# Sigmoid attention and a GELU feed-forward on one core: half of each k load issued on GpSimd's queue instead of SyncE's

## The chip, the core and the metric

The kernel runs on one core of a Trainium2 chip. The metric is device time in microseconds (us) for one execution, and lower is better. A core has TensorE (PE in the profile; its weight loads are a row of their own, PEld), VectorE (DVE), ScalarE (ACT), GpSimd (POOL) and SyncE (SP). Each runs its own instructions in order and waits for the others by semaphores. DMAs are issued on the queue of SP, ACT or POOL, and the transfers of all three are carried by the same 16 DMA engines. In the profile SP's transfers are queue q1, ACT's q10 and POOL's q0.

## The reference

```python
def _attn_ref(q, k, v):                      # each (8, 12, 448, 64), float32
    S = q.shape[2]
    scale = 1.0 / np.sqrt(q.shape[-1])
    scores = scale * np.matmul(q, k.transpose(0, 1, 3, 2)) - np.log(S)
    attn = 1.0 / (1.0 + np.exp(-scores))     # a sigmoid, no softmax
    return np.matmul(attn, v)

x = attn_out.transpose(0, 2, 1, 3).reshape(8 * 448, 768)
h = x @ w_in                                 # (768, 2048)
g = 0.5 * h * (1.0 + erf(h / sqrt(2)))       # exact GELU
out = g @ w_out                              # (2048, 768)
```

## The kernel before, in words

**Two stages.** The attention stage (`attention`) fills the first 240 us or so, and the feed-forward (`feed_forward`), which is the rest, reads attention's result back from a scratch tensor in DRAM, `scr_x`. While attention runs, a `Decoder` unpacks the weights (stored as 64-bit words) a step at a time with VectorE and ScalarE, and writes them to scratch tensors (`scr_f`, later `scr_out`).

**Units.** Attention's work is cut into 24 units, B x NU = 8 batches x 3, each with two pairs of heads. A head pair lies in the 128 partitions: head j = 0 in partitions 0 to 63, head j = 1 in 64 to 127. One tile `qk` holds a unit's q and k (`raw[:, pp, 0]` is q and `raw[:, pp, 1]` is k), and there are three such buffers. So the load of unit u + 3 can start only when unit u's buffer has been read for the last time.

**One unit on the engines.** `scores` multiplies k by q on TensorE into PSUM (line 380; from unit 1 on as three products of high and low parts), and `sigmoid` turns each of six chunks into a tile `a` on ScalarE (line 358). `values` multiplies `a` by v (line 413), computes the last 64 keys of the *next* unit on the way (`scores_tail`, line 397, which reads `qk` as loaded), and goes on with the values. `park` copies the result to a tile `x` on VectorE (line 452) and stores it to `scr_x` on POOL (line 455). The high and low parts are made from `qk` as it was loaded: the high part by `high_qk` on ScalarE up to unit 17 for the first head pair, otherwise on VectorE (line 341), the low part on VectorE (line 350).

**What sets the order.** The scheduling is by hand: each engine runs its instructions in the order in which the program issues them. Before the loop come `load(0)`, `load_v(0)`, `load(1)`, `load_v(1)`, `load(2)`. Then each round of the loop over u issues, in this order: the scores of unit u, `load(u + 3)`, the splits of unit u + 1 (`split_qk`), a few decoder steps, the values of unit u with the tail scores of unit u + 1 and ScalarE's split of unit u + 2 (`idle`), more decoder steps inside it, `park`, and `load_v(u + 2)`.

**The queues around the change.** `load(u)` (lines 320 and 324) issues q in one DMA of 448 KB for both pairs, and k in two of 224 KB, one for each half of the partitions (j = 0 and j = 1). All three go on SP, but for unit 0, whose loads are cut by pair and whose j = 0 half of k goes on ACT. On SP they stand in order with v's loads (line 333) and the decoder's loads of raw weights (line 114); late in attention also with loads of the decoded weights (line 243). POOL issues the decoder's stores (`scr_f`, line 156), the stores of `x` (line 455) and, once, after unit 16, four loads that bring the first part of `scr_x` back for the feed-forward (`load_x`, tile `xl`, line 286). POOL computes nothing in attention.

Of the kernel before, what the change touches and what calls it, by code (L numbers as in the profile page):

```python
# [21 lines left out]
def tile_sigmoid_attention_gelu_ffn(  # L22
# [10 lines left out]
    nc = tc.nc  # L33
# [240 lines left out]
    def rows(j):  # L274
        return slice(j * D, j * D + D)
# [31 lines left out]
    def attention(at, ps):  # L307
# [3 lines left out]
        def load(u):  # L311
            if u >= total:
                return
            b, n = divmod(u, NU)
            raw = at.tile([P, 2, 2, S], F32, tag="qk", name=f"qk{u}", bufs=3)
            for pp in (slice(0, 1), slice(1, 2)) if u == 0 else (slice(0, 2),):
                if u == 0 and pp.start == 1:
                    nc.scalar.activation(one, one, AF.Sigmoid)
                hps = slice(2 * n + pp.start, 2 * n + pp.stop)
                nc.sync.dma_start(raw[:, pp, 0], q[b, hps].rearrange("p r s -> r p s"))  # L320
                for j in range(2):
                    src = k[b, hps, rows(j), j].rearrange("p r s -> r p s")
                    queue = nc.scalar if j == 0 and u == 0 else nc.sync
                    queue.dma_start(raw[rows(j), pp, 1], src)
            raws[u] = raw

# [139 lines left out]
        for i in range(10):  # L466
            nc.tensor.matmul(warm[:, 0], ready[:, :P], ready, start=True, stop=True)  # L467
        load(0)
        load_v(0)
        load(1)  # L470
        load_v(1)
        load(2)
        for u in range(total):
            for p in range(2):
# [415 lines left out]
```

## Time and profile before

| what | value |
|---|---|
| time, median of 3 runs | 1024.78 us (1024.43 to 1025.58) |
| the profiled execution | 1025.23 us |
| its span, first to last instruction | 1023.5 us |
| mean granted TensorE clock | 1.000 |
| PE busy | 1019.0 us (100%) |
| PEld busy | 922.4 us (90%) |
| DVE busy | 785.7 us (77%) |
| ACT busy | 605.0 us (59%) |
| POOL busy | 116.7 us (11%) |
| SP's queue (q1) | 153.82 MB, 49.9% of 16 DMA engines' span |
| POOL's queue (q0) | 55.26 MB, 15.0% |
| ACT's queue (q10) | 1.72 MB, 0.5% |

How to read it: the span is the part of the execution from the first to the last instruction. The ends of matmuls are modelled, so PE's busy time says that TensorE always had work in hand and not that it ran at its peak; where it waited is seen better in PEld's rows. In the lists of waits, a row gives who waited, for whom, the total time, how often, and the longest. In the timeline, a row gives start and duration, the engine, the line and the operation, `out<-in`, and in brackets the idle time before it and what ended that. A name with q at its end, as SPq, is the engine's queue, that is, its sequencer issuing a DMA: the duration is that of the issue, not of the transfer. "To landing" is from the issue to the last byte.

### The profile page before, as it was taken

What the parts mean: (1) busy time and instruction counts of PE and PEld (TensorE: products, weight loads), DVE (VectorE), ACT (ScalarE), POOL (GpSimd) and SP (SyncE); (2) the same over time, 40 slices, a digit from 0 to 9 for tenths busy, and PEclk for the clock granted to TensorE, in tenths of its full rate; (3) what the DMA queues carried; (4) which work ended last, traced back from release to release, by engine and by line L of the source; (5) the groups of instructions that cost most, each with busy time, mean ns of one, the idle gap of its engine ahead of it and who ended that gap; (6) DMA issues with size and microseconds to landing.
All of it is one profiled execution on the core that took longest, in us unless ns stands there. A gap on an engine that the chain in (4) does not pass through costs nothing.

```text
span 1023.5 us, 16634 instructions
## 1 busy us (share of the span) xinstructions
PE 1019.0 (100%) x6478; PEld 922.4 (90%) x6478; DVE 785.7 (77%) x1011; ACT 605.0 (59%) x804; POOL 116.7 (11%) x186
## 2 busy tenths in 40 slices
PE   9999999999999999999999999999999999999998
PEld 5656666567999999999999999999999999999998
DVE  3678777885799698996688888566888875678875
ACT  5888887784445465555366645635655455466552
POOL 0111102101323362224000000100000000000000
PEclk9999999999999999999999999999999999999999
DMA  9999999996788797688444445634444553334441
GB/s 259 290 326 319 310 326 301 349 284 228 236 259 272 265 340 261 215 282 322 158 143 126 147 123 161 220 107 140 131 114 133 163 166 100 117 115 133 139 138 64
DMA packets 85935, 211.87 MB, mean 207 GB/s; under 512 B 9376, under 2 KB 35872, under 8 KB 85856
## 3 DMA queue, kind: packets, MB, share of 16 engines
q1 hardware_dynamic: 69072, 153.82, 49.9%
q0 software_dynamic: 14880, 55.26, 15.0%
q10 hardware_dynamic: 1904, 1.72, 0.5%
q8 instruction: 51, 0.84, 0.3%
q14 instruction: 28, 0.23, 0.1%
HBM read 163.38 MB, written 50.33 MB: 209 GB/s over the span
## 4 chain that ended last, share of the span: by engine, by line
PE 100%; DVE 0%; DVEq 0%; issue 0%
PE pf L525 76%; PE pav L413 12%; PE sc L380 9%; PE sc_t L397 2%; PE pav L428 0%; PE warm L467 0%; DVE tmp L562 0%; DVEq L886 0%
## 5 line engine op out<-in xcount | busy, mean ns | idle before, releaser
L525 PE MATMUL pf<-op,whl 128*128 128x448 f32 x2016 | 382.8, 353 | 0.0
L525 PEld LDWEIGHTS pf<-op,whl 128*128 128x128 f32 x2016 | 380.3, 189 | 1.8 <-DVE op L562 0.8
L254 ACT CAST whl<-wst 128x768 fp32r<-128x768 f32 x212 | 176.4, 833 | 241.8 <-PE pf L525 210.4
L525 PE MATMUL pf<-xh_p,whl 128*128 128x448 f32 x1008 | 273.4, 352 | 0.0
L261 DVE TENSOR_TENSOR whl<-wst,whl 128x768 fp32r<-128x768 f32 x212 | 201.8, 953 | 47.1 <-ACT whl L254 46.9
L525 PEld LDWEIGHTS pf<-xh_p,whl 128*128 128x128 f32 x1008 | 190.5, 189 | 0.2
L525 PE MATMUL pf<-xl_p,whl 128*128 128x448 f32 x504 | 177.6, 352 | 0.0
L358 ACT ACTIVATE a<-sc 128x896 f32<-128x896 f32 x144 | 119.3, 934 | 33.4 <-PE sc L380 33.4
L413 PE MATMUL pav<-a,v 64*64 64x448 f32 x1296 | 132.8, 541 | 0.0
L562 DVE TENSOR_TENSOR op<-g,op 128x896 fp32r<-128x896 f32 x112 | 121.4, 1085 | 5.8 <-ACT op L572 5.7
L413 PEld LDWEIGHTS pav<-a,v 64*64 64x64 f32 x1296 | 55.2, 132 | 61.2 <-issue 34.5
L572 ACT CAST op<-g 128x896 fp32r<-128x896 f32 x112 | 104.6, 935 | 2.6 <-PE pf L525 2.6
L525 PE MATMUL pf<-xh,whl 128*128 128x448 f32 x384 | 104.2, 353 | 0.0
L525 PEld LDWEIGHTS pf<-xl_p,whl 128*128 128x128 f32 x504 | 95.3, 189 | 0.0
L525 PEld LDWEIGHTS pf<-xh,whl 128*128 128x128 f32 x384 | 72.6, 189 | 0.8 <-issue 0.7
L562 DVE TENSOR_TENSOR g<-g,g 128x896 f32<-128x896 f32 x64 | 69.4, 1084 | 0.0
L525 PE MATMUL pf<-xl,whl 128*128 128x448 f32 x192 | 67.7, 352 | 0.0
L559 ACT ACTIVATE g<-tmp 128x448 f32<-128x448 f32 x72 | 45.2, 628 | 35.8 <-DVE tmp L562 35.8
L562 DVE TENSOR_TENSOR tmp<-pf,g 128x448 f32<-128x448 f32 x72 | 44.9, 624 | 27.2 <-PE pf L525 26.4
L562 DVE TENSOR_TENSOR g<-pf,g 128x448 f32<-128x448 f32 x48 | 29.9, 624 | 34.6 <-PE pf L525 34.5
L380 PE MATMUL sc<-lo,hi 64*128 64x448 f32 x276 | 51.2, 367 | 0.0
L133 ACT ACTIVATE me<-me 128x512 f32<-128x512 int32 (+1 forms) x40 | 29.5, 738 | 36.6 <-DVE me L122 36.6
(78 smaller groups left out, 910.0 us busy)
## 6 DMA issues: line engine op xcount, KB each, us to landing
wst<-scr_out SPq DMA_DIRECT2D x112, 384.0 KB, 3.2
wst<-scr_in SPq DMA_DIRECT2D x84, 384.0 KB, 3.1
v<-v_dram SPq DMA_DIRECT2D x24, 512.0 KB, 6.9
raw<-w_in_dram SPq DMA_DIRECT2D x16, 768.0 KB, 5.0
raw<-w_out_dram SPq DMA_DIRECT2D x24, 512.0 KB, 5.5
scr_x<-x POOLq DMA_DIRECT2D x24, 448.0 KB, 7.6
out_dram<-tmp SPq DMA_DIRECT2D x47, 224.0 KB, 2.3
qk<-q_dram SPq DMA_DIRECT2D x23, 448.0 KB, 9.7
```

The costliest lines, as they stand in the source:

```text
L133: nc.scalar.activation(e.bitcast(F32), e.bitcast(I32), AF.Relu, bias=1151.0 * 2**23, scale=-8.0)
L254: nc.scalar.copy(hl[:, 0], t)
L261: nc.vector.tensor_tensor(hl[:, 1], t, hl[:, 0], op=ALU.subtract)
L358: nc.scalar.activation(to, sc, AF.Sigmoid, bias=NEG_LOG_S, scale=SCALE)
L380: nc.tensor.matmul(sc[:, j], ks[rows(j), 1, keys], braid(qs[rows(j), 0]) if braided else qs[rows(j), 0], start=n == 0, stop=n == last,)
L397: nc.tensor.matmul(sc[rows(p), j], raw[rows(j), p, 1, FULL * P :], raw[rows(j), p, 0], start=True, stop=True,)
L413: nc.tensor.matmul(pav[rows(j), p], vals[u][half, p, j, c], a[p][half, j], start=not swap and c == order[0], stop=c == (order[-1], FULL - ...
L525: nc.tensor.matmul(bank, a, braid(m), **flags)
L559: nc.scalar.activation(straight(dst), unbraid(src), AF.Gelu)
L562: nc.vector.tensor_tensor(out, a, b, op=op)
L572: nc.scalar.copy(op[:, 0], src)
```

## The change

From unit 1 on, the j = 1 half of k (partitions 64 to 127, both head pairs, 224 KB) is issued on POOL's queue and not on SP's. Its place in the program, its bytes, its source and its destination are the same. Unit 0 keeps its queues: j = 0 on ACT and j = 1 on SP. q, the j = 0 half of k, and v stay on SP.

```diff
                 nc.sync.dma_start(raw[:, pp, 0], q[b, hps].rearrange("p r s -> r p s"))
                 for j in range(2):
                     src = k[b, hps, rows(j), j].rearrange("p r s -> r p s")
-                    queue = nc.scalar if j == 0 and u == 0 else nc.sync
+                    queue = (nc.scalar, nc.sync) if u == 0 else (nc.sync, nc.gpsimd)
+                    queue = queue[j]
                     queue.dma_start(raw[rows(j), pp, 1], src)
             raws[u] = raw
```

## The prediction

> **What bounds the kernel now.** I read the busy totals and the chain first, then the waits of the attention stage, then one middle unit, and last the start, where the queues fill.
>
> ```profile
> PE 1019.0 (100%) x6478; PEld 922.4 (90%) x6478; DVE 785.7 (77%) x1011; ACT 605.0 (59%) x804; POOL 116.7 (11%) x186
> PE 100%; DVE 0%; DVEq 0%; issue 0%
> PE pf L525 76%; PE pav L413 12%; PE sc L380 9%; PE sc_t L397 2%; PE pav L428 0%; PE warm L467 0%; DVE tmp L562 0%; DVEq L886 0%
> ```
>
> The chain that ended last is TensorE from end to end. A changed DMA moves the time only if it makes TensorE wait, or ends a wait that TensorE has. The moved loads end with attention, so the rows that count are the waits of the first 240 us:
>
> ```profile
> ACT a L358 <- PE sc L380: 33.4, 24, 3.9
> DVE x L452 <- PE pav L413: 23.5, 19, 2.9
> PEld pav L413 <- ACT a L358: 14.5, 64, 0.3
> DVE hi L341 <- DMA qk<-k_dram: 1.0, 1, 1.0
> PEld sc L380 <- DMA qk<-k_dram: 0.7, 1, 0.7
> ACT hi L341 <- DMA qk<-k_dram: 0.7, 1, 0.7
> ```
>
> Columns: who, whom, total us, times, longest. TensorE waited for q or k once, 0.7 us, and that was unit 0 (its row is below), whose loads the change leaves alone. The other two waits are of VectorE and ScalarE, which themselves idle 23.5 and 33.4 us for TensorE. So k's lateness costs nothing now, and the gain to be had from it is about nothing.
>
> One middle unit, whose scores begin at 86.17:
>
> ```profile
> 86.17 3.60 PE sc L380 x36
> 95.98 3.60 PE sc L380 x36
> 84.79 0.93 ACT L341 CAST hi<-qk 128x896 fp32r<-128x896 f32 x1
> 86.98 4.97 ACT L358 ACTIVATE a<-sc 128x896 f32<-128x896 f32 x6 [1.26 <-PE sc L380]
> 85.66 1.44 SPq L324 DMA_DIRECT2D qk<-k_dram  x2
> 85.54 0.56 POOL L156 DMA_DIRECT2D scr_f<-wd  x1 [6.92 <-DVE wd L147]
> 87.71 0.71 POOL L455 DMA_DIRECT2D scr_x<-x  x1 [1.61 <-DVE x L452]
> 86.26 1.16 DVE L452 COPY x<-pav 128x448 f32<-128x448 f32 x2 [1.02 <-PE pav L413]
> 88.33 0.62 DVE L341 CAST hi<-qk 128x896 fp32r<-128x896 f32 x1
> ```
>
> The period is 95.98 - 86.17 = 9.81 us, set by the scores, sigmoid, values circle; SP and POOL only have to be in time.
>
> **The change part by part.** It adds and removes no bytes. 23 of the 46 k loads of 224 KB go from SP's queue to POOL's, each past SP's v, raw and q issues, and behind POOL's `scr_f`, `scr_x` and, once, x0's loads.
>
> *SP, per unit.* One issue of about 0.72 us (1.44 for two) less. SP is not on the chain: 0.
>
> *POOL, per unit.* In program order the moved load stands behind the store of the unit before, so it is issued at 87.71 + 0.71 = 88.4 and not at about 86.4, 2 us later. Its own wait, for the third-last `qk` buffer, ends earlier: that buffer's last readers are the tail scores and splits before 86.17. So nothing is held up behind it: the next POOL item, `scr_f`, comes 9.81 us after 85.54, and POOL's 6.92 us idle ahead of that takes an issue of 0.57 to 0.71 us.
>
> *When k lands.*
>
> ```profile
> scr_x<-x POOLq DMA_DIRECT2D x24, 448.0 KB, 7.6
> qk<-k_dram SPq DMA_DIRECT2D x46, 224.0 KB, 10.5
> DMA to landing us min/median/max: 3.0/7.5/11.8
> q1 hardware_dynamic: 82, 0.45, 54.2%
> q0 software_dynamic: 77, 0.41, 49.3%
> q1 hardware_dynamic: 265, 0.43, 107.0%
> ```
>
> The third row is of all transfers of `scr_x`. The fourth and fifth are the queues in 24 to 26 us (packets, MB, share of the engines), SP's q1 beside POOL's q0; the last is q1 alone in 9 to 11 us. The store ahead lands 7.6 us after 87.71, at 95.3; 224 KB more at POOL's 0.41 MB in 2 us take 1.1 us: 96.4. SP's second half now lands at about 86.4 + 10.5 = 96.9. The first use is ScalarE's split of that unit, two periods after 84.79: 104.4. Slack 8 us; by the longest landing (88.4 + 11.8 + 1.1 = 101.3) still 3. Cost 0.
>
> *The worst unit.* x0's loads go out on POOL ahead of unit 20's k:
>
> ```profile
> 176.72 3.05 POOL L286 DMA_DIRECT2D xl<-scr_x  x4
> 177.29 0.63 DVE L341 CAST hi<-qk 128x896 fp32r<-128x896 f32 x1
> 178.97 0.55 DVE L122 TENSOR_SCALAR me<-raw 128x768 uint32<-128x768 uint32 x1
> 195.26 0.62 DVE L341 CAST hi<-qk 128x896 fp32r<-128x896 f32 x1
> 195.91 1.09 DVE L350 TENSOR_TENSOR lo<-qk,hi 128x896 fp32r<-128x896 f32 x1
> 203.84 0.19 PEld L380 LDWEIGHTS sc<-lo,hi 64*128 64x128 f32 x2 [0.70 <-issue]
> ```
>
> It is issued at 179.8 and by that longest landing is there at 192.7; VectorE splits it at 195.26, and its scores begin at 203.84. Slack 2.6 us to the split, and then 8.6 less 3.4 for the two splits (0.62 and 1.09 twice) to TensorE. Cost 0.
>
> *VectorE beside POOL's issues.* Four issues in 3.05 us ran beside a cast of 0.63 us, where the undisturbed one at 195.26 took 0.62, and were not slowed either: 0.76 each, against 0.71 for `scr_x`. The moved issue falls beside the cast at 88.33. Cost 0; the cover is the 1.02 us that VectorE idles before its next copy, and without it the issue's 0.71 us in 21 units would be 15 us.
>
> [...]
>
> *The start.* POOL has nothing to wait for there, so the second halves of units 1 and 2 (2 x 224 KB) go out at once, beside unit 0's loads, where SP sends them after unit 0.
>
> ```profile
> 0.74 0.40 SPq L320 DMA_DIRECT2D qk<-q_dram  x1
> 0.74 0.56 ACTq L324 DMA_DIRECT2D qk<-k_dram  x1
> 7.66 1.40 SPq L324 DMA_DIRECT2D qk<-k_dram  x2
> 4.59 1.25 PEld L380 LDWEIGHTS sc<-qk 64*128 64x128 f32 x5 [0.73 <-DMA qk<-k_dram]
> 10.37 0.21 PEld L397 LDWEIGHTS sc_t<-qk 64*64 64x64 f32 x8 [0.65 <-ACT a L358]
> 2.94 0.59 SPq L333 DMA_DIRECT2D v<-v_dram  x1
> v<-v_dram SPq DMA_DIRECT2D x1, 512.0 KB, 7.0
> 11.17 3.19 PE L413 MATMUL pav<-a,v 64*64 64x448 f32 x32
> 17.37 3.77 PE sc L380 x36
> ```
>
> TensorE already waits here, 0.73 us, for unit 0's k; what delays that load delays all. The engines can't be late by more than POOL's packets occupy them: 0.41 MB took 49.3% of 2 us, 0.99 us, so 448 KB (0.459 MB) take 1.10 us; if POOL's k goes in the small packets of SP's loads, by the 107% of 2 us for 0.43 MB, 2.3 us. Lower end 0: POOL's data may come after unit 0's first pair. Not below: all that is moved was queued behind that pair. Later waits of unit 0 add nothing: v lands at 9.9, 1.2 us ahead of its use at 11.17, and the second pair is covered by ScalarE, for which TensorE waits 0.65 us at 10.37. What SP loses (224 KB ahead of unit 1, at 0.43 MB in 2 us 1.07 us) pays back POOL's time by unit 1, but TensorE's shift stays. Between 0 and 2.3 I take 0.6, half the 1.10: the large packets are what POOL's row shows, and with both queues starting at once about half of them should fall ahead of the first pair.
>
> **Sum.** +0.6 us at the start, 0 elsewhere. The profiled execution took 1025.23 (span 1023.5 and 1.7 around it) and would take 1025.8; the median of the three runs, 1024.78, is 0.45 lower, so 1025.4.
>
> **The rivals.**
> Hidden altogether: POOL's first data come after unit 0's. For it: a store issued on POOL beside a full SP queue takes 7.6 us. Time 1024.8, on the same side of what a measurement can tell (0.2%, 2.05 us).
>
> Slower by the start: POOL's k goes in small packets, all ahead of the first pair. It decides above 2.05 us, so only at its end of 2.3: 1027.1. Against it: POOL's 77 packets carried 0.41 MB, 5.3 KB each, while q1's 265 carried 1.6 KB.
>
> Slower by late k: beyond its slack k makes ScalarE's split late, which pushes the sigmoids. Each us beyond the 8 of slack and the 1.26 that ScalarE idles costs 21 us over 21 units, 1046. It needs landings of 17 us; the longest on POOL was 11.8.
>
> Faster: with less queued on SP, the early loads land sooner. The 1.0 and 0.7 us waits on k go, but neither engine is on the chain; TensorE's own 0.7 us is unit 0's. At most 1024.1. Over 0.2% would need 2.05 us of TensorE waiting for loads, and the list has 0.7. Against: the 14.5 us that it waits for ScalarE, if those hang on loads by a path I don't see; a seventh of it gone gives 1022.7.
>
> [...]
>
> **How the numbers follow.** Forecast, a start cost of 0.1 to 2.05 us: 0.50. Hidden: 0.37. Slower by the start beyond 2.05: 0.07. Late k: 0.03. Faster: 0.03. Faster, same, slower: 0.03, 0.87, 0.10. The range runs from 1024.0, the lowest run 1024.43 less about its spread, to the start's upper end, 1027.1.
>
> **What would show it.** SP's k groups of one load instead of two; POOL issuing two k loads before 3 us; unit 1's scores later than 17.37 by up to 1 us; the period still 9.81; the splits' waits on k gone; the feed-forward unchanged. It is wrong if the period moves, if ScalarE's or VectorE's waits for k grow past a few us, or if TensorE gets a row of waits for `qk` after unit 0.

## The result, and the profile after

The change makes the kernel slower. The median of six runs went from 1025.13 to 1031.01 us (1029.47 to 1033.82), a ratio of 1.0059 with a 95% interval of 1.0049 to 1.0069. One of the six runs before took 5377.27 us; the ratio leaves it out, and the other five have a median of 1024.79. The profiled execution of the changed kernel took 1030.97 us with a span of 1029.2, against 1025.23 and 1023.5. Line numbers behind the edit are one higher than in the kernel before.

The page of the changed kernel gives the busy totals, and the chain that ended last by engine and line:

```profile
PE 1021.3 (99%) x6478; PEld 922.1 (90%) x6478; DVE 786.6 (76%) x1011; ACT 605.1 (59%) x804; POOL 131.6 (13%) x209
PE pf L526 73%; PE pav L414 12%; PE sc L381 8%; PE sc_t L398 2%; DMA xl<-scr_x 1%; DMA qk<-q_dram 1%; DMA scr_out<-s 1%; PE pav L429 0%; DVE xl L290 0%; ACTq L286 0%; DVE s L96 0%; ACT xh L289 0%; DVE s L95 0%; DVE s L98 0%; DVE whl L261 0%
```

POOL has its 23 further DMAs (209 instructions, not 186). The chain is no longer TensorE alone. It leaves TensorE twice: once for a load of q, and once through `xl<-scr_x`, the sums `s`, a store `scr_out<-s` and `whl`. Here is the chain in order of time, some rows of many (start, duration, what):

```profile
1.82 6.90 DMA qk<-q_dram
...
18.60 3.77 PE sc L381 x36
...
87.42 3.60 PE sc L381 x36
...
97.23 3.60 PE sc L381 x36
...
263.18 0.63 POOL scr_out L170
263.81 5.66 DMA scr_out<-s
...
269.55 0.70 DVE s L95
...
272.17 0.88 DVE whl L261
273.10 11.98 PE pf L526 x53
```

Unit 1's scores start at 18.60, where they stood at 17.37: 1.23 us later. The middle unit starts at 87.42 (86.17 before), and its period is 97.23 - 87.42 = 9.81, as before. So one part of the loss is made at the start and is carried along unchanged. Setting the starts of TensorE's instructions of both traces side by side, the shift is +1.24 us from unit 1 to the end of attention and on into the feed-forward. At one place, 269.61 us in the trace of before and 273.10 here, it jumps to +3.49, and by 274 us of before it has grown to +5.09, where it stays. What comes after TensorE's last work adds some 0.6, which makes the 5.7 of the two spans. That part differs between executions anyway (run k below, whose TensorE has no shift, has 0.48 more there than the kernel before), so it isn't put down to the change.

**What happens at 273.** The feed-forward's weights need a last step on VectorE (line 261 makes `whl`), and that stands behind VectorE's sums for the decoder's second half (`mix`, lines 95 to 98, into the one buffer `s`). Four POOL stores read `s`, and the next group's first sum must wait until the last of them has landed. These are the lists of waits from 236 to 280 us, a row of before and then the same of after:

```profile
DVE s L95 <- DMA scr_out<-s: 2.0, 1, 2.0
```

```profile
DVE s L95 <- DMA scr_out<-s: 4.6, 1, 4.6
```

In the kernel before, VectorE had `whl` ready shortly ahead of its use, as its rows show:

```profile
265.67 0.69 DVE L95 TENSOR_TENSOR s<-wd 128x512 f32<-128x512 f32 x1 [1.98 <-DMA scr_out<-s]
268.20 0.95 DVE L261 TENSOR_TENSOR whl<-wst,whl 128x768 fp32r<-128x768 f32 x1
269.61 0.19 PEld L525 LDWEIGHTS pf<-xh,whl 128*128 128x128 f32 x1
```

268.20 + 0.95 is 269.15, and the first load of these weights is at 269.61. The slack was 0.46 us. A TensorE that never waits gives no sign of it. In the changed kernel the same two instructions of VectorE, and TensorE's wait:

```profile
269.55 0.69 DVE L95 TENSOR_TENSOR s<-wd 128x512 f32<-128x512 f32 x1 [4.62 <-DMA scr_out<-s]
272.09 0.95 DVE L261 TENSOR_TENSOR whl<-wst,whl 128x768 fp32r<-128x768 f32 x1
273.10 0.19 PEld L526 LDWEIGHTS pf<-xh,whl 128*128 128x128 f32 x1 [2.24 <-DVE whl L261]
```

`whl` is 3.89 us later, 1.24 of which is the start's shift that TensorE shares; the other 2.65 less the 0.46 of slack leave 2.19 us of waiting, and the row has 2.24. Then TensorE's clock fell. This is the table by windows, whose columns are window, length, busy time and count of PE, PEld, DVE, ACT and POOL, granted clock, DMA share and GB/s:

```profile
271.00:273.00 2.00, 0.20 (x2) 0.00 (x0) 2.00 (x4) 0.00 (x0) 1.50 (x3) 1.00 0.51 145
273.00:275.00 2.00, 1.90 (x6) 1.77 (x7) 1.97 (x5) 1.51 (x3) 1.65 (x3) 0.66 0.89 243
275.00:277.00 2.00, 2.00 (x7) 1.77 (x6) 1.93 (x4) 1.19 (x3) 0.49 (x1) 0.50 1.00 371
```

Granted 0.66 and 0.50 in two windows of 2 us, TensorE lost about 2 x (0.34 + 0.50) = 1.7 us more. By the starts, 3.49 - 1.24 = 2.25 us of waiting and 5.09 - 3.49 = 1.60 of clock make the jump of 3.85.

**Why the store was late.** Here are POOL's issues around the first group of sums, in the kernel before and in the changed one. The stores are counted from the first that reads `s`; two of the group, from `wd`, go ahead of it, and the fifth is from `wd` again:

```profile
258.99 1.45 POOL L170 DMA_DIRECT2D scr_out<-s  x2 [10.65 <-issue]
260.61 1.45 POOL L170 DMA_DIRECT2D scr_out<-s  x2 [0.16 <-issue]
269.81 1.46 POOL L170 DMA_DIRECT2D scr_out<-s  x2 [1.71 <-DVE me L122]
```

```profile
259.97 1.45 POOL L170 DMA_DIRECT2D scr_out<-s  x2 [10.35 <-issue]
263.18 1.45 POOL L170 DMA_DIRECT2D scr_out<-s  x2 [1.77 <-DVE me L126]
272.47 1.45 POOL L170 DMA_DIRECT2D scr_out<-s  x2 [0.48 <-DVE s L98]
```

Before, stores 3 and 4 of the first group follow stores 1 and 2 after 0.16 us, and the second group has an idle time of 1.71. After, it is the reverse: 1.77 us in the first group, 0.48 in the second. The releaser that the rows name, `me`, is no input of these stores: their data, line 98's, were there at about 261.3, as the chain has it. So something holds one store for 1.2 to 1.6 us beyond its usual idle time (1.71 - 0.48 and 1.77 - 0.16), in both kernels, and the change moved it from a harmless store to a dear one. The hold of 1.6 us is not the whole delay: store 4 behind it took 5.66 us to land, and 4.20 in the kernel before.

**The count.** Give each POOL DMA, for each of the 16 DMA engines, its contiguous pieces over 16 and one more: a half of k has 128 pieces of 1792 bytes, 8 + 1 = 9; a store of `s` has 512, 32 + 1 = 33. Summed from the start of the program, the store held in the kernel before takes the sum from 1015 to 1048, and the store held in the changed one from 991 to 1024. The 23 moved loads add 23 x 9 = 207, and seven stores of 33, 231, is how far the hold went forward. The "one more" stands in the trace: of the packets of the kernel before, 9376 are under 512 bytes, 16 for each of its 586 DMAs, as many as there are engines. And SP's queue, with 23 halves of k less, has 69072 - 65760 = 3312 packets less, 144 for each, which is 16 x 9. On POOL's queue a half of k is 64 packets (16352 - 14880 = 1472 for the 23), so the sum is one of pieces and not of the packets that POOL's DMAs show; that this sum is what counts was the author's assumption, for the runs to test. Without the one more the held store of before starts at 960, the one held in run c below ends at 944, and no one limit fits both. The expectations call the units of the sum descriptors. The limit of 1024 is read off the traces here.

### The profile page after: what moved, and what is told of

The parts are those of the page before. It is cut to its first block, busy times and chain, and to the rows that moved or that the text cites. A ratio compares the mean times of both kernels' runs of the same rounds, so it can differ in the third digit from the quotient of the medians.

```text
span 1029.2 us, 16687 instructions
## 1 busy us (share of the span) xinstructions
PE 1021.3 (99%) x6478; PEld 922.1 (90%) x6478; DVE 786.6 (76%) x1011; ACT 605.1 (59%) x804; POOL 131.6 (13%) x209
## 2 busy tenths in 40 slices
DMA packets 84096, 211.87 MB, mean 206 GB/s; under 512 B 9376, under 2 KB 32928, under 8 KB 84016
## 3 DMA queue, kind: packets, MB, share of 16 engines
q1 hardware_dynamic: 65760, 148.54, 47.5%
q0 software_dynamic: 16352, 60.54, 16.4%
## 4 chain that ended last, share of the span: by engine, by line
PE 96%; DMA 2%; DVE 1%; issue 0%; ACTq 0%; ACT 0%; SPq 0%; POOL 0%; DVEq 0%
PE pf L526 73%; PE pav L414 12%; PE sc L381 8%; PE sc_t L398 2%; DMA xl<-scr_x 1%; DMA qk<-q_dram 1%; DMA scr_out<-s 1%; PE pav L429 0%; DVE xl L290 0%; ACTq L286 0%; DVE s L96 0%; ACT xh L289 0%; DVE s L95 0%; DVE s L98 0%; DVE whl L261 0%
## 5 line engine op out<-in xcount | busy, mean ns | idle before, releaser
L351 DVE TENSOR_TENSOR lo<-qk,hi 128x896 fp32r<-128x896 f32 x46 | 50.1, 1089 | 1.1
```

The costliest lines, as they stand in the source:

```text
L351: nc.vector.tensor_tensor(lo, raw, hi, op=ALU.subtract)
```

## The experiments

Three theories stood. *Count*: the hold falls on the POOL DMA that reaches 1024 by that sum, and costs when that is store 3 of the first group. *Phase*: the start's 1.24 us pushes the stores against something that runs beside them. *VectorE*: the held store waits for an operation of VectorE, for which the rows' releaser speaks (`me`, 1.71 and 1.77 us). All medians are set against runs of the kernel before on the same chip; the lines in each diff replace the edit's.

**a: only units 1 and 2 on POOL.** It keeps the start's burden and takes the later loads away.

```diff
-queue = (nc.scalar, nc.sync) if u == 0 else (nc.sync, nc.gpsimd)
+queue = (nc.scalar, nc.sync) if u == 0 else (nc.sync, nc.gpsimd if u < 3 else nc.sync)
```

> Only units 1 and 2 issue the second half of k on POOL; the later units keep SP. Time before: 1025.1 us. Theory 1 (two separate costs: the early POOL loads delay unit 0's second head pair by 1.24 us, and, apart from that, one POOL store at the start of the feed-forward is held up because it is the one whose transfer descriptors pass the 1024th on each DMA engine): the start cost alone, 1026.3; the 1024th now falls on the second store of the second group of sums, where nothing waits closely. Theory 2 (TensorE's lateness of 1.24 us is what breaks the order at the start of the feed-forward): both costs, about 1030. [...]

Measured: 1026.87 us (1026.37 to 1027.89) against 1025.12, ratio 1.0017 (1.0009 to 1.0026). TensorE's shift is +1.14 us after the start and +1.12 behind the first groups. The hold sits in the second group, at 269.32 with 1.27 us of idle time, and `whl` costs nothing. With the start's shift and no loss at 270, the phase does not make the loss. The start alone is worth 1.75 us of the medians (0.9 to 2.7 by the interval).

**b: POOL from unit 3 on.** The complement of a.

```diff
-queue = (nc.scalar, nc.sync) if u == 0 else (nc.sync, nc.gpsimd)
+queue = (nc.scalar, nc.sync) if u == 0 else (nc.sync, nc.gpsimd if u > 2 else nc.sync)
```

> Units 1 and 2 keep SP; from unit 3 on the second half of k goes on POOL. Theory 1: no start cost; 21 loads of 9 descriptors on each engine move the 1024th to the fourth store of the first group of sums, one store later than in the changed kernel, so a hold of about 1.5 us and most of the 3.9 us at the start of the feed-forward stay: 1027 to 1030. Theory 2: no lateness, so no loss: 1025.1. [...]

Measured: 1027.26 us (1024.94 to 1028.06) against 1025.12, ratio 1.0017 (1.0008 to 1.0026). The hold is on store 4 of the first group:

```profile
261.64 0.72 POOL L170 DMA_DIRECT2D scr_out<-s  x1 [1.29 <-issue]
```

In the profiled execution it cost nothing: VectorE's wait was 1.8 us, and TensorE's shift stayed at -0.7 throughout. But that execution was b's shortest, and seven of its eleven took 1027.1 to 1028.1. Their loss, some 2 us, has no trace. So b shows that the start's loss is absent without units 1 and 2; for the rest it is inconclusive.

**c: the change, with 23 tiny DMAs added on POOL.** Each is 128 pieces of 8 bytes, the count of a half of k and next to none of its bytes. It puts the count off by as much again.

```diff
+            if u > 0:
+                pad = at.tile([P, 2], F32, tag="pad", name=f"pad{u}", bufs=8)
+                nc.gpsimd.dma_start(pad, q[b, 0][:, :2])
             raws[u] = raw
```

> The changed kernel with, in every unit from 1 on, one more POOL DMA of 128 runs of 8 bytes (into a tile that nobody reads), issued right behind k. Theory 1: 207 descriptors more on each engine bring the 1024th into attention's last units, on a store of x that nothing waits for; the hold at the start of the feed-forward is gone and only the start cost stays: 1026.4, and one store of x starts some 1.5 us after what it waits for. [...]

**d: the kernel before, with the same 23 tiny DMAs.** No k is moved.

> The kernel before (all of k on SP from unit 1 on) with the same 23 small POOL DMAs of 128 runs of 8 bytes. It has as many POOL DMAs and descriptors as the changed kernel and moves none of k. Theory 1: the 1024th falls on the third store of the first group, as in the changed kernel; no start cost; the loss at the start of the feed-forward comes, 1027.5 to 1030. Theory 2: nothing is late: 1025.1. A theory 4 (k's bytes on POOL's queue are what hurts): 1025.1.

Measured: c took 1026.77 us (1025.19 to 1027.37) against 1025.12, ratio 1.0014 (1.0005 to 1.0023); d took 1027.28 (1025.56 to 1029.75), ratio 1.0027 (1.0018 to 1.0036). In c the store of `x` ahead of the groups is held, and the group's stores follow at once:

```profile
228.87 0.74 POOL L459 DMA_DIRECT2D scr_x<-x  x1 [11.18 <-DVE hi L345]
236.62 0.73 POOL L459 DMA_DIRECT2D scr_x<-x  x1 [7.01 <-DVE x L456]
262.62 1.45 POOL L170 DMA_DIRECT2D scr_out<-s  x2 [0.16 <-issue]
```

The first of these stores is about 2.0 us late: 7.75 us ahead of the next, where the same two stores are 234.88 - 225.16 = 9.72 apart in the kernel before.

In d, whose k loads are all on SP, POOL, VectorE and TensorE show the changed kernel's loss (POOL's row, VectorE's, and one of the list of waits):

```profile
261.73 1.45 POOL L170 DMA_DIRECT2D scr_out<-s  x2 [1.77 <-DVE me L126]
268.02 0.69 DVE L95 TENSOR_TENSOR s<-wd 128x512 f32<-128x512 f32 x1 [4.69 <-DMA scr_out<-s]
PEld pf L528 <- DVE whl L261: 2.3, 1, 2.3
```

d's shift is -0.36 us after the start and +3.56 behind the groups. So the loss at 270 comes without any k moved, and with no shift at the start; and in c it goes although all of k is moved and the start's shift is there (1.70 us). Bytes on POOL's queue, k's lateness and the phase fall as its cause. VectorE falls too: its instructions are the same in c and d, and the hold followed the sum; in b, and in k below, the idle time of the held store is put down to no engine at all (`issue`). d also shows how the cost varies: five of its runs took 1028.8 to 1029.8 with a mean clock of 0.998, and the other six 1025.6 to 1027.3 with the clock near 1.000.

**e: b with c's tiny DMAs.**

> POOL takes the second half of k from unit 3 on (units 1 and 2 keep SP), and the 23 small POOL DMAs of 128 runs of 8 bytes bring the 1024th descriptor into attention's last units. Theory 1 (early loads, and the one held store, are all there is): both costs gone, 1025.1 +- 1, and no wait of TensorE for whl. If k on POOL's queue costs anything by itself in units 3 to 23: above 1026.5.

Measured: 1025.36 us (1024.56 to 1029.85) against 1025.04, ratio 1.0009 (1.0001 to 1.0018). The hold is on a store of `x`, at 236.70 with 10.95 us of idle time.

With units 1 and 2 left on SP, and the hold moved away from the groups, 0.3 us of the loss is left. By the medians the two causes together account for it. One of the twelve runs took 1029.85 us with a mean clock of 0.998; it has no trace, and what made it long is open.

**f: only unit 1 on POOL.** It asks which of the two early loads costs.

```diff
-queue = (nc.scalar, nc.sync) if u == 0 else (nc.sync, nc.gpsimd)
+queue = (nc.scalar, nc.sync) if u == 0 else (nc.sync, nc.gpsimd if u < 2 else nc.sync)
```

> Only unit 1 issues the second half of k on POOL: 224 KB beside unit 0's loads instead of 448. If the start cost is the time that POOL's bytes take from unit 0's loads: about half, unit 1's scores 0.3 to 0.7 us later than before, 1025.4 to 1025.9. If it is a fixed cost of an early POOL DMA: 1.1 us, 1026.3.

Measured: 1026.02 us (1025.2 to 1028.33) against 1025.04, ratio 1.0015 (1.0006 to 1.0023): +0.98 by the medians, about half of a's +1.75. Its profiled execution (1027.76) is one of the longest and shows another cost, which the rows of TensorE's first scores tell. They are, in order, of f and of a:

```profile
4.60 5.59 PE L381 MATMUL sc<-qk 64*128 64x448 f32 x12
```

```profile
4.60 3.07 PE L381 MATMUL sc<-qk 64*128 64x448 f32 x12
8.73 0.99 PE L381 MATMUL sc<-qk 64*128 64x448 f32 x3 [1.06 <-DMA qk<-q_dram]
```

The first twelve matmuls took 5.59 us in f and 3.07 in a: they ran at about half pace, and with that the second pair's load came in time. f's weight loads follow each other in pairs 0.75 us apart from 6.95 to 9.94 us, a's 0.38 apart at 9.54 and 9.92. The first record of the full clock in f's trace is at 10.10 us, in a's at 5.27, so the author puts the pace down to the clock and not to a load. With it f's unit 1 is 2.37 us later than before, which says nothing of one load's price. That f's loss is half of a's holds for the medians; the profile neither bears it out nor contradicts it.

**g: c, with POOL's first k held until unit 0's loads have landed.** POOL copies a few elements of unit 0's tile ahead of its first load.

```diff
+            if u == 1:
+                seen = at.tile([P, 2, 2, 1], F32, tag="seen", name="seen", bufs=1)
+                nc.gpsimd.tensor_copy(seen, raws[0][:, :, :, :1])
```

> The changed kernel with the 23 small POOL DMAs, and with one small POOL copy that reads unit 0's q and k ahead of unit 1's load, so that POOL issues nothing until unit 0's loads have landed. If sharing with unit 0's loads is the start cost: gone, 1025.1 +- 1, and unit 0's second pair lands at about 7 us and not at 9. If not: 1026.4, as without the hold.

Measured: 1026.54 us (1025.52 to 1028.0) against 1025.04, ratio 1.0015 (1.0007 to 1.0024). The expected gain did not come. Unit 0 was as it had been, its scores in one run from 4.53 to 9.75 (24 matmuls). But unit 1's k was then issued at 7.79, and TensorE's tail scores of unit 1 waited for it:

```profile
7.79 0.74 POOL L328 DMA_DIRECT2D qk<-k_dram  x1 [0.39 <-issue]
15.65 0.14 PEld L404 LDWEIGHTS sc_t<-qk 64*64 64x64 f32 x3 [2.03 <-DMA qk<-k_dram]
```

Issued at once, POOL's k stood beside a landing of unit 0's q in 5.0 us instead of 4.0 (the rows of the start, below); held back, it cost unit 1 these 2.03 us. The cost moved from unit 0 to unit 1. The profile has a second, smaller cost: TensorE waits 0.55 us for `whl` at 271.69, with no store of the group held. VectorE's wait ahead of the second group was 2.92 us there, so a slack of 0.46 is lost by less than a hold.

**h: the kernel before with 8 tiny DMAs of three to four times the pieces.** 208 on the sum in 8 DMAs, so that the sum reaches 1024 at POOL's 57th DMA, where d's does at the 72nd. It tells the sum from the number of DMAs.

```diff
+            if 0 < u < 9:
+                n_run = 4 if u == 8 else 3
+                pad = at.tile([P, 4, 2], F32, tag="pad", name=f"pad{u}", bufs=8)
+                runs = q[b, 0][:, : 4 * 8].rearrange("p (n w) -> p n w", w=8)
+                nc.gpsimd.dma_start(pad[:, :n_run], runs[:, :n_run, :2])
```

> The kernel before with 8 small POOL DMAs (seven of 128 x 3 runs of 8 bytes, one of 128 x 4) in units 1 to 8: 208 descriptors more on each engine, but 8 DMAs more and not 23. If the count of descriptors (runs by 16, and one for each DMA) decides which store is held: the third store of the first group again, held by about 1.5 us, 1027.3 as with 23 pads. If it is the number of DMAs or of POOL's instructions: the hold falls elsewhere or not at all, 1025.1.

Measured: 1026.3 us (1025.8 to 1029.4) against 1025.04, ratio 1.0014 (1.0005 to 1.0022). The hold is on store 3 of the first group, and in the profiled execution (1029.4) TensorE waits 2.8 us for `whl`:

```profile
261.73 1.47 POOL L170 DMA_DIRECT2D scr_out<-s  x2 [1.43 <-DVE me L126]
```

The place is the sum's. The size is not as expected: most runs lost about 1.3 us, less than the profiled 4.2.

**The change once more,** for the size of the loss in another execution.

> The changed kernel once more, beside the next run on the same chip: 1029.5 to 1033, in the profile the hold on the third store of the first group of sums, and TensorE's wait for whl.

Measured: 1029.75 us (1028.93 to 1033.09) against 1024.9, ratio 1.0055 (1.0043 to 1.0068). The same store is held, idle 1.77 us, and TensorE waits 2.3 us for `whl`, but in the three windows behind that its clock stays at 1.00. The shift goes from +1.52 to +3.91, a jump of 2.4 us where the first profile had 3.85. There 1.60 of it was the clock, so the waiting costs 2.2 to 2.4 us in both.

**k: POOL from unit 6 on.** By the sum, the hold falls on the fifth store of the first group, from `wd`, for which VectorE's sums don't wait.

```diff
-queue = (nc.scalar, nc.sync) if u == 0 else (nc.sync, nc.gpsimd)
+queue = (nc.scalar, nc.sync) if u == 0 else (nc.sync, nc.gpsimd if u > 5 else nc.sync)
```

> POOL takes the second half of k from unit 6 on: no load of POOL's beside unit 0, and 162 descriptors more on each engine than before, by which the 1024th falls on the fifth store of the first group, which comes from the decoded tile and not from the tile s that the next group writes again. If the hold hurts through the reuse of s: the hold is there (about 1.3 us) and costs nothing, 1025.1 +- 1. If a hold anywhere in the first group hurts: about 1027.3, as with unit 3 on, where it falls on the fourth store.

Measured: 1025.41 us (1024.83 to 1026.73) against 1024.9, ratio 1.0007 (0.9998 to 1.0016). The hold is there and TensorE's shift is 0.0 throughout:

```profile
263.04 2.19 POOL L170 DMA_DIRECT2D scr_out<-wd  x3 [0.93 <-issue]
```

No version was faster than the kernel before. The places of the hold, together (idle time is the one ahead of the issue; the wait is VectorE's at line 95 ahead of the second group):

| kernel | sum reaches 1024 in | idle, us | VectorE's wait, us |
|---|---|---|---|
| before | second group, store 3 (1015 to 1048) | 1.71 | 1.98 |
| after, and again | first group, store 3 (991 to 1024) | 1.77 | 4.62, 4.67 |
| d | first group, store 3 (991 to 1024) | 1.77 | 4.69 |
| h | first group, store 3 (992 to 1025) | 1.43 | 5.21 |
| b | first group, store 4 (1006 to 1039) | 1.29 | 1.80 |
| k | first group, store 5, from `wd` (1012 to 1045) | 0.93 | 2.11 |
| a | second group, store 2 (1000 to 1033) | 1.27 | 1.55 |
| f | second group, store 2 (991 to 1024) | 1.25 | 2.06 |
| c, g | a store of `x` (1015 to 1032) | 11.18, 11.26 | 2.12, 2.92 |
| e | a store of `x` (1014 to 1031) | 10.95 | 1.90 |

Every held DMA begins at a sum of at most 1015 and ends at 1024 or more, so one limit between 1016 and 1024 fits all.

## Why the prediction was wrong, point by point

The forecast was 1025.4 us, between 1024.0 and 1027.1; the measured time was 1031.01.

**The step that failed.** It is "The moved loads end with attention, so the rows that count are the waits of the first 240 us" and, with it, "*POOL, per unit.*", which found nothing held up behind the moved load. What POOL had issued in attention was felt after it, by the sum above: 207 more on it moved the hold seven stores forward, onto store 3 of the first group at 263, and the slack behind it was 0.46 us. This term was taken as 0, and it measured 3.85 us in one profile and 2.4 in the other. c and d show it from both sides, and e and k show the change's later loads without it. "The feed-forward unchanged" was wrong by the same step. Nor did any rival name this path: all of them looked for the loss or the gain in attention's loads.

**The start: right place, size too small.** The loss was forecast at 0.6 us, between 0 and 2.3. It was 1.24 and 1.52 in the two profiles of the change, 1.14 in a's, and 1.75 by a's medians. The profiles are set against one execution of the kernel before, whose start was slow: the six profiles with an unchanged start, this one among them, have unit 1 up to 0.9 us earlier, 0.4 in the mean, and against that mean the four with both early loads (those three, and c's with 1.70) are 1.8 us late, as the medians have it. The sub-step that failed is "the second pair is covered by ScalarE". TensorE's rows of the start, of before and then of after:

```profile
4.60 5.20 PE L380 MATMUL sc<-qk 64*128 64x448 f32 x21
```

```profile
4.49 1.02 PE L381 MATMUL sc<-qk 64*128 64x448 f32 x2
5.99 2.52 PE L381 MATMUL sc<-qk 64*128 64x448 f32 x10 [0.48 <-DMA qk<-k_dram]
8.81 0.99 PE L381 MATMUL sc<-qk 64*128 64x448 f32 x3 [0.30 <-DMA qk<-q_dram]
```

Before, the scores of both pairs run without a break. After, TensorE waits 0.48 us for k of the first pair and 0.30 for q of the second, whose transfer is the first row of the chain above: it landed at 1.82 + 6.90 = 8.72. Unit 0's loads by pair took longer on SP's and ACT's queue, as the issues of the first 3.2 us show (KB each, median us to landing), of before and then of after:

```profile
qk<-q_dram SPq DMA_DIRECT2D x2, 224.0 KB, 4.0
qk<-k_dram ACTq DMA_DIRECT2D x2, 112.0 KB, 4.3
```

```profile
qk<-q_dram SPq DMA_DIRECT2D x2, 224.0 KB, 5.0
qk<-k_dram ACTq DMA_DIRECT2D x2, 112.0 KB, 5.2
```

The medians rose by 1.0 and 0.9 us. The mis-sized term is the half of POOL's 1.10 us that was put ahead of unit 0's data: the cost was all of the 1.10 and more.

**What was right.** SP issues one half of k per unit, and POOL issues two loads before 3 us. The middle units pay nothing. A moved load is issued at 89.66 in the unit shown, straight behind the store of `x`, as worked out (88.4 and the shift of 1.24):

```profile
89.66 0.65 POOL L325 DMA_DIRECT2D qk<-k_dram  x1
196.51 0.62 DVE L342 CAST hi<-qk 128x896 fp32r<-128x896 f32 x1
qk<-k_dram POOLq DMA_DIRECT2D x23, 224.0 KB, 7.7
qk<-k_dram SPq DMA_DIRECT2D x23, 224.0 KB, 10.2
```

It lands 7.7 us after its issue (the last two rows are medians to landing), so at about 97.4, and 96.4 + 1.25 of shift was forecast. Unit 20's split comes at 196.51, 195.26 and the shift, with no wait in it. VectorE's cast took 0.62 us in both kernels. TensorE has no wait for `qk` after unit 0. e and k, with 1025.36 and 1025.41, show the price of 18 to 21 moved loads by themselves: 0.3 and 0.5 us, hardly to be told from nothing. Nor was anything gained by the other issuer: e and k are not below the kernel before, 1025.04 and 1024.9 beside them.

**What stays open.** What the hold is: the runs show its place and its length, not what POOL does in that time. Why the fourth store takes longer to land when the third is held (5.66 us in the chain, 5.58 in d and 6.07 in h, where the four stores of before had a median of 4.2); it is nearly half of the delay. Why most of b's runs were 2 us longer than its profile, and most of h's 3 us shorter than its own, of which the clock explains 1.6. A second buffer for `s`, which would take the wait away, was not tried.

## What to carry to other kernels

Before moving a DMA to another queue, look for the smallest slack anywhere behind that queue to the end of the program, not only in the stage that the DMA serves: where one engine never waits, the chain shows no other, and 0.46 us of slack is invisible until it is gone. Here two early loads on an idle queue, while the first loads were awaited, cost 1.75 us by a's medians, more than the 1.10 us worked out for their bytes, and delaying them moved the cost to the next unit (2.03 us of waiting in g). So count an early load as a cost while others are awaited. When a wait appears far from an edit, add the suspected resource alone (tiny DMAs of the same count) to both kernels: it makes the loss without the edit, and takes it away with the edit in place.

## What the runs showed of the hardware

**A hold on GpSimd's DMAs.** In each of the twelve profiles of this case the POOL DMA that takes the sum, per DMA engine, to 1024 or past it was issued about 0.9 to 2.0 us late. The DMAs that pass 2048 and 3072 in the kernel before, the second `a<-scr_f` of the pair at 345.23 us and the second `x<-scr_x` of the pair at 517.77, were issued with no idle time. The sum is worked out from the kernel's access patterns; what it is that holds 1024, no run here shows.

**The clock after a wait of 2 us.** TensorE waited about 2 us for `whl` in both executions of the change. In the one the clock fell, and in the other it stayed at 1.00. In the profiled execution of the change the clock's records are stretches of full clock of 269.65 and 750.93 us, with one of half clock, 3.413 us, between them; the two are 79 and 220 times as long as that one. The kernel before has one stretch of full clock, 1017.17 us, 298 times as long. In d and h the half clock behind the wait lasted 3.4 us too. Counted off in lengths of 3.413 us, here are the two windows around the wait, first of after and then of its second execution:

```profile
270.21:273.62 3.41, 1.52 (x9) 1.17 (x8) 3.38 (x7) 0.16 (x1) 2.59 (x4) 1.00 0.54 161
273.62:277.03 3.41, 3.41 (x11) 3.04 (x10) 3.29 (x6) 2.57 (x5) 1.55 (x3) 0.50 0.93 310
```

```profile
269.40:272.82 3.42, 2.25 (x12) 1.90 (x11) 2.73 (x5) 0.00 (x0) 1.44 (x2) 1.00 0.62 204
272.82:276.23 3.41, 2.63 (x14) 2.62 (x15) 3.34 (x6) 2.23 (x4) 2.19 (x3) 1.00 0.86 242
```

In the first the whole wait fell into one window, TensorE was busy for 1.52 us of it, and the next window ran at half clock. In the second the wait was parted between two windows, with 2.25 and 2.63 us busy, and nothing happened. In d and h the window ahead of the half clock has 1.45 and 0.98 us busy; a window of g with 2.16 (14.36 to 17.77) was not followed by one. So half clock followed the windows with 0.98, 1.45 and 1.52 us busy, and not those with 2.16, 2.25 and 2.63; in after, 1.9 us without a matmul went ahead of it. What the clock goes by beyond these six windows, no run here shows. One half-clock stretch makes a run's mean clock 0.998 (0.5 x 3.41 of some 1028 us), which is what d's five long runs show, and of h's the profiled one alone.

**The pace of the first matmuls.** Executions whose start is unchanged differ by up to 0.9 us at unit 1. The first scores' rows differ likewise: 21 matmuls in 5.20 us in the kernel before, 24 in 5.15 in b. The first record of the full clock is at 6.25 us in the one and at 4.67 in the other, and in all twelve profiles it lies between 3.51 and 10.10. So two profiles can't size an effect at the start to better than that, and the medians must.
